# Token sums one period later on VectorE, and a subtraction in four pieces on GpSimd, in a spectral block with a GEGLU

## The chip, the cores and the metric

The kernel runs on one core of one Trainium2 chip. The time is that of one execution on the device, in microseconds (us); smaller is better. The profile is of one execution. TensorE is PE in the profile's rows (PEld its weight loads), VectorE DVE, ScalarE ACT, GpSimd POOL, SyncE SP; L12 is line 12 of the kernel of before.

## The reference

What is computed, cut to its core, for 8192 tokens of 448 channels, with six rows (`sa`, `ca`, `ga`, `sb`, `cb`, `gb`) made of one conditioning vector:

```
h = layernorm(x) * (1 + ca) + sa
x = x + ga * spectral(h)        # rfft over the tokens, a two-layer complex MLP in 4 blocks of
                                # channels, soft shrinkage, inverse rfft
h = layernorm(x) * (1 + cb) + sb
x = x + gb * ((gelu(h @ w_gate) * (h @ w_up)) @ w_down)     # 448 -> 1792 -> 448
```

## The kernel before, in words

The first 700 us transform the tokens, apply the spectral MLP and begin the inverse transform. What follows runs over 32 chunks of 256 tokens (`nch`, 2 blocks of 128 each). For each chunk the inverse's last stage is made (`split_v`, `split_g`, `winverse`), the residual is added and the second layernorm is taken (`norm2` writes tile n), then come gate and up products, the gelu times up, and the down product.

Numbers of more than f16's precision are held as a high and a low part, the low one being the number minus its high part: `split` copies the high part on ScalarE and subtracts on GpSimd. For the inverse's input v (128 x 896 of 32-bit floats, 2 blocks of 448) the copy is `vh`, and the subtraction writes the low part over v itself.

The first 8 chunks (`NSTD`) use plain products for gate and up. Chunks 8 to 31 are the new chunks: gate and up are made by a scheme of seven products of sums (as Strassen and Winograd do it), on the tokens' side by `token_sums`, `wpack_hi` and `wpack_lo`, which form the sums of tile n in tile tf and pack high and low parts into pk. `token_sums` has a part 0 (two subtractions on VectorE, L1326 and L1327, and a copy on GpSimd, L1328) and a part 1 (three subtractions on VectorE, L1330 to L1332).

A new chunk has seven periods (k = 0 to 6), one for each pair of 128 hidden features. The order of the work is written out by hand: each engine takes its instructions in program order, and they wait for each other by semaphores. Period u is made by `period(u)`, and three sets of accumulators in PSUM (`sets`) are used in turn, so that stage A of period u writes the set that period u - 3 used. TensorE's order in a period is stage A of period u (32 matmuls), stage D of u - 2 (12), stage C of u - 1 (24) and stage B of u (10), all at L1385. On the other engines, in the order of the period:

- `seed` (ACT L1417) and what is held over from the period before (`held`: the packing, ACT L1356 and POOL L1362);
- `joins` of u - 2 (DVE L1422 and L1428), which read the accumulators that stage D then goes on to write; the first gelu (ACT L1434);
- `quant_lo` of u - 4 (DVE L1460), the gate products `mult3` (DVE L1438), `copy_b` (ACT L1413);
- behind stage D the second gelu (ACT L1442) and the last gate product `mult1` (DVE L1445), which is the last reader of that set of accumulators;
- the sums of the activations (`sums`, POOL L1191 to L1194), and `quant_hi` of u - 3 (ACT L1450), which reads them.

Behind a period stands the chunk's side work of the table `extra`: after k = 0 `split_v` (ACT L114, POOL L116) for the chunk two ahead, after k = 1 `split_g`, after k = 3 and k = 4 the two parts of `token_sums`; packing goes to `held` and so into the period that follows. After k = 2 `phase` puts the inverse and the seven down products (L1215 to L1217) of the chunk before on TensorE; the last add of these on VectorE is L1270, and GpSimd's are L1229, L1230 and L1261. Weights of the gate and up products come by DMA from SP in each period (L1301).

Of the kernel before, what the change touches and what calls it, by code (L numbers as in the profile page):

```python
# [10 lines left out]
F32 = mybir.dt.float32  # L11
# [5 lines left out]
ALU = mybir.AluOpType  # L17
# [7 lines left out]
CB = 2  # L25
# [15 lines left out]
NSTD = 8  # L41
# [8 lines left out]
def spectral_geglu(ctx, tc, x, w1, b1, w2, b2, wg, wu, wd, cvec, wmod, cf1, cs2, cmi, cgm, out):  # L50
    nc = tc.nc
    V, S, G, T = nc.vector, nc.scalar, nc.gpsimd, nc.tensor
# [59 lines left out]
    def split(hi, lo, src, eh=None, el=None):  # L112

        (eh or S.copy)(hi, src)  # L114
        h = hi.bitcast(F32) if hi.dtype == F32R else hi
        (el or V).tensor_tensor(lo, src, h, ALU.subtract)  # L116
# [883 lines left out]
    with ExitStack() as cctx:  # L1000
# [14 lines left out]
        def each(i):  # L1015

            return [slice(b, b + 1) for b in range(CB)] if i == 0 else [slice(0, CB)]


        halves = [slice(0, HC), slice(HC, D)]  # L1020

        def split_v(i, cs=slice(0, D)):
            n = nxt[i]
            if "vh" not in n:
                n["vh"] = cp.tile([128, CB, D], F32R, tag="vh", name="vh")
                n["vl"] = n["v"].bitcast(F32R)
            for b in each(i):
                split(n["vh"][:, b, cs], n["vl"][:, b, cs], n["v"][:, b, cs], el=G)

# [159 lines left out]
        def sums(x, e):  # L1189
            a12, a11, s1, s2, a22, s3, s4, a21 = (x[:, j] for j in range(8))  # L1190
            e.tensor_tensor(s1, a21, a22, ALU.add)  # L1191
            e.tensor_tensor(s2, s1, a11, ALU.subtract)  # L1192
            e.tensor_tensor(s3, a11, a21, ALU.subtract)  # L1193
            e.tensor_tensor(s4, a12, s2, ALU.subtract)  # L1194
# [82 lines left out]
        NT_, U0 = nch * NP, NSTD * NP  # L1277
# [27 lines left out]
        def after(u, part):  # L1305

            if u in refill:
                pending.append((refill[u], part))

        def flush(keep=()):  # L1310

            for u, part in [p for p in pending if p[1] not in keep]:
                load_part(u, part)
                pending.remove((u, part))
# [84 lines left out]
        def stage_b(u):  # L1399
            mm(u, RY, S2, T2)  # L1400
# [10 lines left out]
        def copy_b(u):  # L1411
            sbs[u] = cp2.tile([128, 2, 256], F32, tag="sb", name="sb", bufs=2)
            S.copy(sbs[u], sets[u % 3][:, :, 0:256])  # L1413
# [50 lines left out]
        def on(u, f):  # L1464
            if U0 <= u < NT_:
                f(u)

        held = []

        def period(u):  # L1470
            on(u, stage_a)
            if u == U0:
                copy_b(u)
                return
            if u == U0 + 1:
                stage_b(U0)
                copy_b(u)
            on(u - 1, seed)
            for fn, *args in held:
                fn(*args)  # L1480
            held.clear()
            on(u - 2, joins)
            on(u - 2, gel3)
            on(u - 4, quant_lo)
            on(u - 2, mult3)
            if u != U0 + 1:
                on(u, copy_b)
            on(u - 2, stage_d)
            on(u - 2, lambda v: after(v, 1))
            on(u - 2, gel1)  # L1490
            on(u - 2, mult1)
            on(u - 2, lambda v: sums(xs[v], G))
            on(u - 3, quant_hi)
            if u == U0 + 1:
                stage_b(u)
                after(U0, 0)
            on(u - 1, stage_c)
            if u != U0 + 1:
                on(u, stage_b)
            on(u, lambda v: after(v, 0))  # L1500
# [12 lines left out]
        def phase(i):  # L1513

            u = i * NP + LA
            pf = sets[(u + 1) % 3]
            j = i + 2
            on(u - 3, quant_lo)
            if j < nch:
                winverse(j, pf)  # L1520
                residual(j)
            steps = {
                0: [(stats2,), (rsqrt_part, 5)],
                1: [(rsqrt_part, 9), (norm2, 0)],
                2: [(norm2, 1)],
            }

            def mid(n):
                for fn, *args in steps[n] if j < nch else []:
                    fn(j, *args)  # L1530

            down(i - 1, down_banks(pf), mid)

        extra = {
            0: [(2, split_v)],
            1: [(2, split_g), (1, wtransposes, [0])],
            2: [(1, wtransposes, range(1, 5))],
# [135 lines left out]
        for n, k in enumerate((4, 7, 11, 13)):  # L1673
# [3 lines left out]
        hooks = {  # L1677
            5: [(1, turn)],
            1: [(2, split_g), (2, split_v)],
            6: [(2, inverse)],  # L1680
            7: [(2, residual)],
# [8 lines left out]
        def later_by_one(k):  # L1690
# [14 lines left out]
        soon = {  # L1705
            0: [(1, token_sums, 0), (1, token_sums, 1), (1, wpack_hi, range(3)), (1, wpack_lo, range(3))],
            1: [(1, wpack_hi, [3, 4]), (1, wpack_lo, [3, 4]), (2, split_g), (2, split_v)],
            5: [(1, turn)],
            6: [(2, inverse)],
# [58 lines left out]
        def store_out():  # L1768
            for i, x1 in outs:
                dma(ov[:, i * CB : (i + 1) * CB, :], x1)  # L1770
            outs.clear()
# [73 lines left out]
        for u in range(U0, NT_ + 1):  # L1845
            period(u)
            i, k = divmod(u, NP)
            if i == nch:
                continue
            if k == LA + 2:  # L1850
                store_out()
            flush()
            for d, fn, *args in opening[k] if i == NSTD and k < 3 else extra[k]:
                if i + d < nch:
                    if fn in (wpack_hi, wpack_lo):
                        held.append((fn, i + d, *args))
                    else:
                        fn(i + d, *args)
            if k == LA:
                phase(i)  # L1860
# [82 lines left out]
```

## Time and profile before

| what | value |
|---|---|
| median of 3 runs | 1890.91 us (1890.71 to 1893.4) |
| the profiled execution's own time | 1890.96 us |
| its span, first to last instruction | 1889.2 us |
| mean granted TensorE clock | 0.996 |
| TensorE busy | 1848.9 us, 98% |
| VectorE, ScalarE, GpSimd busy | 1429.5, 994.4, 1266.7 us |
| DMA | 330.49 MB, 175 GB/s over the span |

In a group's row stand the line, the engine, the operation, the output and inputs by the program's names, the count after an x, then busy time in us and the mean of one in ns, then the engine's idle time before them and what ended it. In a row in order of time stand the start and the duration in us first; a bracket at its end gives idle time ahead of it and what released it.

### The profile page before, as it was taken

To read this page: it belongs to the slowest core of one execution; us is meant where nothing else is said; L and a number is where in the kernel's file an instruction comes from. 1 tells how busy PE (TensorE), PEld (TensorE's weight loads), DVE (VectorE), ACT (ScalarE), POOL (GpSimd) and SP (SyncE) were. 2 spreads that over 40 slices of the span, in tenths; PEclk is the share of its full clock that TensorE was granted. 3 is DMA by queue.
4 is the path that set the end of the run, shared out by engine and by line. 5 is a ranking of instruction groups with operands and counts; after the bars stand their busy time and mean duration, and the time that the engine had idled before them with its cause. 6 is when DMAs were issued, how large, how long until landed. Compare 5 with 4: busy or idle time off the path is not lost.

```text
span 1889.2 us, 56357 instructions
## 1 busy us (share of the span) xinstructions
PE 1848.9 (98%) x23332; PEld 1751.7 (93%) x23332; DVE 1429.5 (76%) x2887; ACT 994.4 (53%) x1844; POOL 1266.7 (67%) x1618
## 2 busy tenths in 40 slices
PE   7899999999999999999999999999999999999998
PEld 3599999878889899999999999999999999999998
DVE  8678788777766667777777777777777777777655
ACT  5677888653444444454554555544554455444443
POOL 3157654347777778777777777777777777777534
PEclk9999999999999999999999999999999999999999
DMA  9999777654544445966666666666666666666651
GB/s 353 316 298 264 205 177 193 185 160 95 133 103 98 99 93 127 296 176 170 169 168 168 168 168 168 168 168 170 177 174 173 169 174 176 176 174 168 162 163 55
DMA packets 380614, 330.49 MB, mean 175 GB/s; under 512 B 110784, under 2 KB 358724, under 8 KB 380356
## 3 DMA queue, kind: packets, MB, share of 16 engines
q1 hardware_dynamic: 380356, 326.87, 63.5%
q8 instruction: 183, 3.00, 0.7%
q14 instruction: 75, 0.61, 0.1%
HBM read 243.32 MB, written 60.10 MB: 161 GB/s over the span
## 4 chain that ended last, share of the span: by engine, by line
PE 77%; DVE 9%; DMA 4%; issue 3%; ACT 3%; POOL 2%; SPq 2%; ACTq 0%; POOLq 0%; DVEq 0%
PE set L1385 34%; PE pgu L1142 10%; PE pdn L1217 6%; PE pdn L1215 6%; PE pdn L1216 6%; PE set L1217 2%; PE set L1216 2%; PE set L1215 2%; DMA xt<-in_A_x 2%; PE ps L211 1%; DVE y L479 1%; DVE x L1438 1%; DVE c L1422 1%; DVE tf L1326 1%; POOL yl L116 1%
## 5 line engine op out<-in xcount | busy, mean ns | idle before, releaser
L1385 PE MATMUL set<-nt,wk 128*128 128x128 f16 x13104 | 742.9, 219 | 3.7 <-DMA wk<-wk 1.6
L1385 PEld LDWEIGHTS <-wk 128*128 128x128 f16 x13104 | 735.6, 98 | 8.9 <-issue 4.8
L1217 PE MATMUL pdn<-wd,ac 128*128 128x224 f16 x1218 | 315.5, 259 | 0.6 <-DVE ac L1203 0.6
L1215 PE MATMUL pdn<-wd,ac 128*128 128x224 f16 x1218 | 315.7, 259 | 0.0
L1216 PE MATMUL pdn<-wd,ac 128*128 128x224 f16 x1218 | 315.5, 259 | 0.0
L1142 PE MATMUL pgu<-nt,wk 128*128 128x256 f16 (+1 forms) x2464 | 269.0, 274 | 3.3 <-DVE x L1183 3.3
L1142 PEld LDWEIGHTS <-wk 128*128 128x128 f16 (+1 forms) x2464 | 226.1, 98 | 44.7 <-issue 18.8
L1434 ACT ACTIVATE gl<-c,dg 128x384 f32<-128x384 f32 x168 | 103.4, 616 | 255.2 <-DVE c L1428 254.2
L1460 DVE SCALAR_TENSOR_TENSOR ac<-x,sa_act,ac 128x896 f16<-128x896 f32 x168 | 212.2, 1263 | 14.7 <-ACT ac L1450 14.7
L1191 POOL TENSOR_TENSOR x<-x 128x128 f32<-128x128 f32 x223 | 130.4, 585 | 120.2 <-DVE x L1183 57.7
L1261 POOL TENSOR_TENSOR cq<-cq 128x224 f32<-128x224 f32 x32 | 21.0, 657 | 262.6 <-DVE cq L1260 262.6
L1438 DVE TENSOR_TENSOR x<-c,gl 128x384 f32<-128x384 f32 x168 | 177.0, 1054 | 17.0 <-ACT gl L1434 17.0
L1450 ACT ACTIVATE ac<-x,sa_act 128x896 f16<-128x896 f32 x168 | 173.5, 1033 | 4.0 <-DVE x L1194 1.3
L1194 POOL TENSOR_TENSOR x<-x 128x128 f32<-128x128 f32 x223 | 170.0, 762 | 0.0
L1215 PEld LDWEIGHTS <-ac 128*128 128x128 f16 x1568 | 153.4, 98 | 4.9 <-issue 4.8
L1217 PEld LDWEIGHTS <-ac 128*128 128x128 f16 x1568 | 153.4, 98 | 0.8 <-DVE ac L1203 0.8
L1216 PEld LDWEIGHTS <-ac 128*128 128x128 f16 x1568 | 153.5, 98 | 0.1
L1193 POOL TENSOR_TENSOR x<-x 128x128 f32<-128x128 f32 x223 | 148.5, 666 | 0.0
L1422 DVE TENSOR_TENSOR c<-set,sb 128x512 f32<-128x512 f32 x168 | 114.9, 684 | 36.1 <-PE set L1385 36.1
L1178 ACT ACTIVATE gel<-pgu,dg 128x256 f32<-128x256 f32 x112 | 49.4, 470 | 158.0 <-PE pgu L1142 150.4
L479 DVE SCALAR_TENSOR_TENSOR y<-pm,t 64x224 f32<-64x224 f32 x256 | 99.5, 389 | 39.1 <-ACT t L471 35.5
L1192 POOL TENSOR_TENSOR x<-x 128x128 f32<-128x128 f32 x223 | 116.9, 524 | 17.5
(336 smaller groups left out, 3987.1 us busy)
## 6 DMA issues: line engine op xcount, KB each, us to landing
wk<-wk SPq DMA_DIRECT2D x76, 1024.0 KB
wk<-wk SPq DMA_DIRECT2D x76, 768.0 KB
vd<-us SPq DMA_DIRECT2D x64, 224.0 KB
xx<-in_A_x SPq DMA_DIRECT2D x32, 448.0 KB
v<-vd SPq DMA_DIRECT2D x63, 224.0 KB
out<-x SPq DMA_DIRECT2D x31, 448.0 KB
xt<-in_A_x SPq DMA_DIRECT2D x15, 896.0 KB
tr<-td SPq DMA_DIRECT2D x60, 224.0 KB
```

Of the source, the lines that this page charges most:

```text
L1142: T.matmul(pgu[i, t, q][:, pr * H : (pr + 1) * H], ws[rows, n, w, tw], nts[i][rows, tn, :], start=start, stop=stop, skip_group_check=True,)
L1191: e.tensor_tensor(s1, a21, a22, ALU.add)
L1193: e.tensor_tensor(s3, a11, a21, ALU.subtract)
L1194: e.tensor_tensor(s4, a12, s2, ALU.subtract)
L1215: T.matmul(ps, ac[:, 0, ka], w[:, 0, kb], start=n == 0, stop=False)
L1216: T.matmul(ps, ac[:, 0, ka], w[:, 1, kb], start=False, stop=False)
L1217: T.matmul(ps, ac[:, 1, ka], w[:, 0, kb], start=False, stop=n == NP - 1)
L1385: T.matmul(ps2[:, pr, reg * 128 : reg * 128 + 128], slot[:, pr, hl, wt, :], nt[:, xt, :], start=start and j == 0, stop=j == len(terms) - 1 ...
L1422: V.tensor_tensor(c[:, :, 1:3, :], p[:, :, 0:256].rearrange("p g (r c) -> p g r c", r=2), b[:, :, 0:128].rearrange("p g (o c) -> p g o c", ...
L1438: V.tensor_tensor(xs[u][:, 1::3, :], cts.pop(u)[:, 1], gls.pop(u), ALU.mult)
L1450: S.activation(ac[:, 0], xs[u][:, 0:7], AF.Copy, scale=sa_act[:, t : t + 1])
L1460: V.scalar_tensor_tensor(ac[:, 1], xs.pop(u)[:, 0:7], sa_act[:, t : t + 1], ac[:, 0], op0=ALU.mult, op1=ALU.subtract)
```

## The change

Two edits, both for the new chunks alone. The two parts of `token_sums` are no longer put behind the period after which `extra` names them, but into a list, `trail`, that the next period empties behind its joins and its gate products, ahead of its sums. The first new chunk's opening is left as it was. And for chunks from 10 on, `split_v` subtracts in four GpSimd instructions of 224 columns (2 blocks times 2 halves) where it had one of 896; the copy to `vh` stays one.

```
@@ split_v
+            if i > NSTD + 1:
+                S.copy(n["vh"], n["v"])
+                for b in range(CB):
+                    for c in halves:
+                        G.tensor_tensor(n["vl"][:, b, c], n["v"][:, b, c], n["vh"][:, b, c].bitcast(F32), ALU.subtract)
+                return
             for b in each(i):
                 split(n["vh"][:, b, cs], n["vl"][:, b, cs], n["v"][:, b, cs], el=G)
@@ period
-        held = []
+        held, trail = [], []
...
             on(u - 2, mult1)
+            for fn, *args in trail:
+                fn(*args)
+            trail.clear()
             on(u - 2, lambda v: sums(xs[v], G))
@@ the loop over the periods
-                    if fn in (wpack_hi, wpack_lo):
+                    if fn is token_sums and u > U0:
+                        trail.append((fn, i + d, *args))
+                    elif fn in (wpack_hi, wpack_lo):
                         held.append((fn, i + d, *args))
```

TensorE's, ScalarE's and SP's instructions stand in the same order in both kernels. On VectorE, from the gate products of period 3 of a new chunk on, there stood in the kernel before (c is the joins' output, x the gate products', ac what `quant_lo` writes):

```order
L1438 TENSOR_TENSOR x_21087<-c,gl_21085 128x3x128
L1445 TENSOR_TENSOR x_21087<-set_11305,gl_21103 128x128
L1326 TENSOR_TENSOR tf<-n_20950 128x192
L1327 TENSOR_TENSOR tf<-n_20950 128x192
L1422 TENSOR_TENSOR c<-set_11303,sb 128x2x256
L1428 TENSOR_TENSOR c<-set_11303,sb 128x2x128
L1460 SCALAR_TENSOR_TENSOR ac<-x_20786,sa_act,ac 128x896
L1438 TENSOR_TENSOR x_21195<-c,gl_21192 128x3x128
L1445 TENSOR_TENSOR x_21195<-set_11303,gl_21211 128x128
L1330 TENSOR_TENSOR tf<-n_20950,tf 128x192
L1331 TENSOR_TENSOR tf<-n_20950,tf 128x192
L1332 TENSOR_TENSOR tf<-n_20950 128x64
```

At the same place of VectorE's order in the changed kernel, whose lines are 6 to 12 higher (L1444 and L1451 are the gate products, L1428 and L1434 the joins, L1466 `quant_lo`, L1332 and L1333 part 0 of the token sums):

```order
L1444 TENSOR_TENSOR x_21120<-c,gl_21118 128x3x128
L1451 TENSOR_TENSOR x_21120<-set_11305,gl_21136 128x128
L1428 TENSOR_TENSOR c<-set_11303,sb 128x2x256
L1434 TENSOR_TENSOR c<-set_11303,sb 128x2x128
L1466 SCALAR_TENSOR_TENSOR ac<-x_20819,sa_act,ac 128x896
L1444 TENSOR_TENSOR x_21224<-c,gl_21221 128x3x128
L1451 TENSOR_TENSOR x_21224<-set_11303,gl_21240 128x128
L1332 TENSOR_TENSOR tf<-n_20983 128x192
L1333 TENSOR_TENSOR tf<-n_20983 128x192
L1428 TENSOR_TENSOR c<-set_11304,sb 128x2x256
L1434 TENSOR_TENSOR c<-set_11304,sb 128x2x128
```

Part 0 has moved from ahead of the joins of period 4 to ahead of those of period 5. Right behind those rows, through period 5 and into period 6, VectorE has now (L1336 to L1338 are part 1):

```order
L1466 SCALAR_TENSOR_TENSOR ac<-x_21120,sa_act,ac 128x896
L1444 TENSOR_TENSOR x_21330<-c,gl_21327 128x3x128
L1451 TENSOR_TENSOR x_21330<-set_11304,gl_21346 128x128
L1336 TENSOR_TENSOR tf<-n_20983,tf 128x192
L1337 TENSOR_TENSOR tf<-n_20983,tf 128x192
L1338 TENSOR_TENSOR tf<-n_20983 128x64
L1428 TENSOR_TENSOR c<-set_11305,sb 128x2x256
```

Part 1 has moved from ahead of the joins of period 5 to ahead of those of period 6. On GpSimd, around period 1 of a new chunk, the kernel before had the sums of one period, the subtraction for v, and the sums of the next:

```order
L1194 TENSOR_TENSOR x_22437<-x_22437 128x128
L116 TENSOR_TENSOR v<-v,vh 128x896
L1191 TENSOR_TENSOR x_22539<-x_22539 128x128
L1192 TENSOR_TENSOR x_22539<-x_22539 128x128
L1193 TENSOR_TENSOR x_22539<-x_22539 128x128
```

There the changed kernel has on GpSimd:

```order
L1200 TENSOR_TENSOR x_22473<-x_22473 128x128
L1031 TENSOR_TENSOR v<-v,vh 128x224 x4
L1197 TENSOR_TENSOR x_22578<-x_22578 128x128
L1198 TENSOR_TENSOR x_22578<-x_22578 128x128
L1199 TENSOR_TENSOR x_22578<-x_22578 128x128
```

The one instruction has become four in its place. Part 0's copy on GpSimd (L1328, now L1334) has moved too, from ahead of the three packing subtractions that follow period 3 to behind them.

## The prediction

> **What bounds the kernel now.** I read the page first, then the waits of TensorE in the new chunks (from 760 us on), then the chain, then the rows of one chunk in order of time.
>
> ```profile
> span 1889.2 us, 56357 instructions
> PE 1848.9 (98%) x23332; PEld 1751.7 (93%) x23332; DVE 1429.5 (76%) x2887; ACT 994.4 (53%) x1844; POOL 1266.7 (67%) x1618
> ```
> ```profile
> PE set L1385 <- DMA wk<-wk: 1.6, 1, 1.6
> PE set L1385 <- ACT sb L1413: 0.6, 1, 0.6
> PE set L1385 <- DVE c L1428: 0.6, 1, 0.6
> ```
>
> The second fence is all that TensorE's matmuls are said to wait for after 700 us: three waits, 2.8 us. Yet matmuls overlap, so a short hole between two of them counts as busy. The holes show in how many matmuls fit a stretch. These rows of TensorE in order of time give start, length, and count after the x:
>
> ```profile
> 1212.84 18.36 PE L1385 MATMUL set<-nt,wk 128*128 128x128 f16 x326
> 1205.43 30.99 PE L1385 MATMUL set<-nt,wk 128*128 128x128 f16 x546
> 1210.40 2.38 PE L1385 MATMUL set<-nt,wk 128*128 128x128 f16 x36
> 1184.39 2.42 PE L1385 MATMUL set<-nt,wk 128*128 128x128 f16 x38
> ```
>
> One matmul lasts 0.219 us, so the undisturbed first row gives a pitch of (18.36 - 0.22) / 325 = 55.8 ns. The second row is a whole chunk's seven periods: 545 x 0.0558 + 0.22 = 30.63 us, but it took 30.99, so 0.36 us are holes. The third row should take 35 x 0.0558 + 0.22 = 2.17: **hole A, 0.21 us**. The fourth should take 2.28: **hole B, 0.14 us**. Together they are the 0.36 within rounding. A period has 78 matmuls, 4.35 us; its stage A has 32 of them, 1.79 us.
>
> Hole A, at 1211.6, is in period 4 of the chunk (the one with k = 4; period 3 starts with the first matmul of the second row, 1205.43, period 4 at 1209.78). Stage D there is due at 1209.78 + 1.79 = 1211.57 and needs the joins L1422 and L1428 of that period:
>
> ```profile
> 1208.98 0.28 DVE L1445 TENSOR_TENSOR x<-set,gl 128x128 f32<-128x128 f32 x1
> 1208.71 1.33 POOL L1230 TENSOR_TENSOR x<-cq,x 128x448 f32<-128x448 f32 x1
> 1209.18 1.09 DVE L1326 TENSOR_TENSOR tf<-n 128x192 f32<-128x192 f32 x1
> 1210.19 0.61 DVE L1327 TENSOR_TENSOR tf<-n 128x192 f32<-128x192 f32 x1
> 1210.72 0.68 DVE L1422 TENSOR_TENSOR c<-set,sb 128x512 f32<-128x512 f32 x1
> 1211.32 0.41 DVE L1428 TENSOR_TENSOR c<-set,sb 128x256 f32<-128x256 f32 x1
> ```
> ```profile
> 1211.78 24.64 PE set L1385 x436
> 1251.83 0.39 DVE cq L1270
> ```
>
> The joins end at 1211.73, and the chain goes from them to TensorE at 1211.78. Ahead of them stand the two token sums of part 0, 1.54 us from 1209.18 to 1210.72; L1326 ends at 1210.27, 0.23 after POOL's L1230. The chain's next chunk shows the same place 46.20 us on (its add L1270 at 1251.83 answers to one at 1205.63).
>
> Hole B, at 1185.5, is at the start of period 2. Its stage A writes the accumulators that the last gate product L1445 of period 1 reads:
>
> ```profile
> 1181.79 1.28 DVE L1460 SCALAR_TENSOR_TENSOR ac<-x,sa_act,ac 128x896 f16<-128x896 f32 x1
> 1182.08 2.94 POOL L116 TENSOR_TENSOR v<-v,vh 128x896 fp32r<-128x896 f32 x1
> 1183.00 2.45 DVE L1438 TENSOR_TENSOR x<-c,gl 128x384 f32<-128x384 f32 x1
> 1183.93 0.37 ACT L1442 ACTIVATE gl<-set,dg 128x128 f32<-128x128 f32 x1
> 1185.37 0.28 DVE L1445 TENSOR_TENSOR x<-set,gl 128x128 f32<-128x128 f32 x1
> 1185.52 0.46 POOL L1191 TENSOR_TENSOR x<-x 128x128 f32<-128x128 f32 x1 [0.50 <-DVE x L1438]
> 1212.81 0.59 DVE L1438 TENSOR_TENSOR x<-c,gl 128x384 f32<-128x384 f32 x1
> ```
>
> L1438 takes 0.59 us at 1212.81 and 2.45 here: it ends at 1185.45, 0.43 after the POOL operation on v ends (1185.02). It stood still for that operation. The operation itself waited for L1460 to end at 1183.07, and then ran some 1.95 us. So DVE's and POOL's operations between SBUF tiles exclude each other for their whole length. The Trainium skill states this (SBUF — State Buffer, section Who interferes with whom): a VectorE instruction with two SBUF inputs and a GpSimd one that reads SBUF hold the shared ports for a whole instruction, and the loser blocks. These rows agree.
>
> **The change part by part.** The two groups over the new chunks, and a POOL operation of 224 columns:
>
> ```profile
> L1326 DVE TENSOR_TENSOR tf<-n 128x192 f32<-128x192 f32 x22 | 23.9, 1086 | 0.0
> L116 POOL TENSOR_TENSOR v<-v,vh 128x896 fp32r<-128x896 f32 x21 | 61.8, 2944 | 0.0
> L1261 POOL TENSOR_TENSOR cq<-cq 128x224 f32<-128x224 f32 x22 | 14.5, 657 | 219.4 <-DVE cq L1260 219.4
> ```
>
> *Hole A removed.* Without part 0 ahead of them, the joins of period 4 start when TensorE's stage C is done. In period 6, which starts at 1205.43 + 3 x 4.35 + 0.21 = 1218.70, they start at 1218.34 straight behind PE, 0.36 before the period:
>
> ```profile
> 1218.34 0.69 DVE L1422 TENSOR_TENSOR c<-set,sb 128x512 f32<-128x512 f32 x1 [0.20 <-PE set L1385]
> ```
>
> So in period 4 they run from 1209.42 to 1210.43 (1.01 us for both), 1.1 us before stage D is due. Stage D then waits for nothing but stage A, on TensorE itself. 22 token sums: 22 x 0.208 = **4.6 us off**.
>
> *Where the sums go.* Joins may start up to 1.79 - 1.01 - 0.05 = 0.73 us after their period's start before stage D waits. Part 0 now stands behind the last gate product of period 4, ahead of the joins of period 5; part 1 one period later. The gate product L1445 starts 3.11 us into an undisturbed period (1188.81, in the period that began at 1185.69, which is 1218.70 - 46.20 + 3 x 4.35 + 0.14), so it ends 3.40 in:
>
> ```profile
> 1188.81 0.29 DVE L1445 TENSOR_TENSOR x<-set,gl 128x128 f32<-128x128 f32 x1 [0.21 <-ACT gl L1442]
> 1213.52 0.34 DVE L1330 TENSOR_TENSOR tf<-n,tf 128x192 f32<-128x192 f32 x1
> 1213.89 0.47 DVE L1331 TENSOR_TENSOR tf<-n,tf 128x192 f32<-128x192 f32 x1
> 1214.28 0.69 DVE L1332 TENSOR_TENSOR tf<-n 128x64 f32<-128x64 f32 x1
> 1214.90 0.68 DVE L1422 TENSOR_TENSOR c<-set,sb 128x512 f32<-128x512 f32 x1
> ```
>
> Part 0: from 1209.78 + 3.33 = 1213.11 (the next DVE operation starts 0.07 before an end). At its old 1.54 us the joins of period 5 start at 1214.65; they are due by 1214.13 + 0.73 = 1214.86. Margin 0.21, and the old price held the wait for L1230, which is long over by then; two operations at L1330's 0.34 are the other end, 0.7 us, and I expect about 1.2. Part 1: from 1217.46, at its old 1.38 us (1213.52 to 1214.90), gives 1218.84 against 1218.48 + 0.73 = 1219.21. **Margin 0.37**, the thinnest that rests on an unseen encounter: POOL's work beside it is other than before. The ends: 0.7 us less (no stop at all, and no gain, since TensorE has nothing to gain there), or each of the three stopped for a whole POOL operation:
>
> ```profile
> 1217.48 0.99 POOL L1362 TENSOR_TENSOR pk<-n,pk 128x256 f16<-128x256 f32 x1
> 1218.43 0.45 POOL L1191 TENSOR_TENSOR x<-x 128x128 f32<-128x128 f32 x1
> ```
>
> that is 0.99 + 0.45 + 0.45, and 0.25 us each to run (from L1326's 0.23 behind L1230): 2.64 us, 0.89 late. I take the old price, nearest in kind: cost 0. ScalarE's casts of the tf pieces stand a period behind each part still, and POOL's copy into tf changes places with three pk operations: the same POOL work ahead of the same sums; it is hidden behind TensorE's periods.
>
> *Hole B removed.* The first of four pieces starts when L1460 ends, at 1183.02, and takes about 0.6 us; L1438, asked for at 1183.00, then runs 0.45 and ends near 1184.1. Its follower L1445 then waits only for ScalarE's L1442, 1184.30, and ends at 1184.6, 0.9 us before stage A needs it. 21 x 0.136 = **2.9 us off**. On POOL, four pieces cost 4 x 0.657 = 2.63 in place of some 1.95 to 2.1, and L1438 now runs between them (0.45): the last ends near 1185.8 in place of 1185.02. The 0.50 us that POOL sat idle before L1191 hides about two thirds; the sums, which ended at 1188.18, come some 0.3 us later, and ScalarE takes them at 1188.68. The inverse on TensorE reads v at 1190.31. Cost 0; were that cover gone, ScalarE's copy would come as much later, and nothing on TensorE hangs on it within the period.
>
> ```profile
> 1186.88 1.30 POOL L1194 TENSOR_TENSOR x<-x 128x128 f32<-128x128 f32 x1
> 1188.68 1.03 ACT L1450 ACTIVATE ac<-x,sa_act 128x896 f16<-128x896 f32 x1
> 1190.31 0.19 PEld L1508 LDWEIGHTS set<-v,gh 128*128 128x128 f32 x1
> ```
>
> *Sum.* 4.6 + 2.9 = 7.4 us (unrounded) off the profiled execution, 1890.96 us, whose span is 1889.2; it stands 0.05 over the median of the runs, 1890.91. **1883.5 us.** DMAs, their order on SP, TensorE's and ScalarE's orders stay.
>
> **The rivals.** (1) *The hole moves to period 6*: part 1 makes its joins some 0.2 us late, as hole A was. 22 x 0.2 = 4.4 back: 1887.9. For: POOL's pk operation of 0.99 us and two sums stand just there. Against: a margin of 0.37 at the old price. (2) *Three full stops*: each operation of part 1 meets a POOL operation from its start, 0.89 late: 22 x 0.89 = 19.6, 1903.1. It is slower than before from 0.34 us late on. For: L1327 and L1326 were both stopped. Against: L1330 was not, and three full stops in a row are in no row here. The skill's section named above lets this happen, as it has no share of the port, only a whole instruction. (3) *POOL keeps the port over its four pieces*, so L1438 waits for all, 0.6 + 3 x 0.657 = 2.57 us in place of the single operation's 1.95, 0.62 more: 21 x 0.62 = 13.0 on, 4.6 off: 1899.4. Against it:
>
> ```profile
> 1220.34 0.81 DVE L1438 TENSOR_TENSOR x<-c,gl 128x384 f32<-128x384 f32 x1
> 1220.70 0.77 POOL L1194 TENSOR_TENSOR x<-x 128x128 f32<-128x128 f32 x1
> ```
>
> L1438 runs there among POOL's sums, which follow each other without a break, and the sum behind it takes 0.77 in place of L1191's 0.45. (4) *The split does nothing for hole B*: 1886.4.
>
> **How the numbers follow.** Forecast 0.62; rival (1) 0.18; (2) 0.06; (3) 0.05; (4) 0.09. A measurement of this kernel tells about 0.2%, 3.8 us, from no change: below 1887.1 is faster, above 1894.7 slower. The forecast and (4) are faster, 0.71; (1) is within, 0.18; (2) and (3) are slower, 0.11. The range goes from 1882.8 (both holes slightly larger than read) to 1889.0, which takes in (4) and (1) up to a hole of 0.25 us; what is left out is (2), (3) and the rest of (1).
>
> **What would show it.** Seven periods in one row of 546 matmuls in 30.6 us, and chunks 45.86 us apart in place of 46.20. L1422 of period 4 about 0.36 before its period, with PE as its releaser. L1438 beside the four pieces about 1.1 us in place of 2.45. Joins of period 6 no later than 0.73 us into it: if they are later, rival (1) or (2). A row of 2.28 us for 38 matmuls at the start of period 2; if 2.42 or more, rival (3) or (4). The prediction is wrong if the gaps of TensorE go where I did not look, as at the down products.

## The result, and the profile after

| | before | after |
|---|---|---|
| median of 5 runs | 1891.38 us (1890.71 to 1893.4) | 1883.83 us (1882.79 to 1884.1) |
| the profiled execution | 1890.96 us | 1882.79 us |
| its span | 1889.2 us | 1881.0 us |

The ratio is 0.9958, 95% interval 0.9947 to 0.997: 7.6 us less by the medians, 0.4%, and the interval lies clear of no change. The profiled executions differ by 8.17 us; 0.8 of that lies ahead of the new chunks, whose first matmul started at 761.3 us before and at 760.5 after, where nothing was changed.

The page and the waits of TensorE show next to nothing, as before. These are the page's first two rows and all waits of matmuls after 700 us:

```profile
span 1881.0 us, 56421 instructions
PE 1841.5 (98%) x23332; PEld 1748.9 (93%) x23332; DVE 1397.2 (74%) x2887; ACT 1000.7 (53%) x1844; POOL 1271.3 (68%) x1684
```
```profile
PE set L1391 <- DMA wk<-wk: 1.6, 1, 1.6
PE set L1391 <- ACT sb L1419: 0.6, 1, 0.6
PE set L1391 <- DVE c L1434: 0.6, 1, 0.6
```

The gain is in how closely the matmuls stand. One chunk's seven periods as a row in order of time (start, length, count), and the same chunk in the chain of work, with its neighbour:

```profile
1201.63 30.65 PE L1391 MATMUL set<-nt,wk 128*128 128x128 f16 x546
```
```profile
1155.93 30.48 PE set L1391 x546
1201.79 30.48 PE set L1391 x546
```

30.65 us in place of 30.99: both holes are gone, and chunks follow each other in 1201.79 - 1155.93 = 45.86 us in place of 46.20. The chain says the same in another way. Before, it left TensorE in 14 of the 22 chunks that have hole A, for the last add of the down products and VectorE's joins, gate product and token sums; in the other 8 it shows hole A only as a pause of some 0.04 us. Now it stays on TensorE for all 546 matmuls of every chunk, since nothing else ends last. The same reading of all chunks, by the starts of their matmuls: before, hole A stands in 22 chunks, 0.21 us in the mean, and hole B in 21, 0.13 us, 7.4 us together; after, none of them has a hole.

Hole A's place, period 4 of this chunk (1201.63 + 4.35 = 1205.98), and VectorE behind it:

```profile
1205.63 0.69 DVE L1428 TENSOR_TENSOR c<-set,sb 128x512 f32<-128x512 f32 x1 [0.17 <-PE set L1391]
1206.23 0.41 DVE L1434 TENSOR_TENSOR c<-set,sb 128x256 f32<-128x256 f32 x1
1209.31 0.35 DVE L1332 TENSOR_TENSOR tf<-n 128x192 f32<-128x192 f32 x1
1209.58 0.58 DVE L1333 TENSOR_TENSOR tf<-n 128x192 f32<-128x192 f32 x1
1210.08 0.68 DVE L1428 TENSOR_TENSOR c<-set,sb 128x512 f32<-128x512 f32 x1
1213.66 0.66 POOL L1368 TENSOR_TENSOR pk<-n,pk 128x256 f16<-128x256 f32 x1
1213.66 0.87 DVE L1336 TENSOR_TENSOR tf<-n,tf 128x192 f32<-128x192 f32 x1
1214.57 0.50 DVE L1337 TENSOR_TENSOR tf<-n,tf 128x192 f32<-128x192 f32 x1
1214.99 0.47 DVE L1338 TENSOR_TENSOR tf<-n 128x64 f32<-128x64 f32 x1
1215.39 0.68 DVE L1428 TENSOR_TENSOR c<-set,sb 128x512 f32<-128x512 f32 x1
```

The joins of period 4 start 0.35 us before their period, and what they waited for is TensorE (the bracket). Part 0 takes 0.77 us (1209.31 to 1210.08). Part 1 takes 1.73 (1213.66 to 1215.39), and the joins behind it start 0.70 us into period 6 (1201.63 + 3 x 4.353 = 1214.69).

Hole B's place, period 1 (GpSimd's four pieces are merged into one row):

```profile
1223.98 1.42 DVE L1466 SCALAR_TENSOR_TENSOR ac<-x,sa_act,ac 128x896 f16<-128x896 f32 x1
1224.42 3.70 POOL L1031 TENSOR_TENSOR v<-v,vh 128x224 fp32r<-128x224 f32 x4
1225.33 1.02 DVE L1444 TENSOR_TENSOR x<-c,gl 128x384 f32<-128x384 f32 x1
1226.52 0.29 DVE L1451 TENSOR_TENSOR x<-set,gl 128x128 f32<-128x128 f32 x1 [0.17 <-ACT gl L1448]
```

The gate product beside the pieces takes 1.02 us where it took 2.45. The last gate product now waits for ScalarE and ends at 1226.81, 0.95 us before period 2 (1201.63 + 6 x 4.353 = 1227.75). Behind the pieces, the last of GpSimd's sums of period 2, and ScalarE's `quant_hi` right behind it:

```profile
1230.49 0.45 POOL L1200 TENSOR_TENSOR x<-x 128x128 f32<-128x128 f32 x1
1230.97 1.04 ACT L1456 ACTIVATE ac<-x,sa_act 128x896 f16<-128x896 f32 x1
```

### The profile page after: what moved, and what is told of

Same layout as the page of the kernel before. It is cut to its first block, busy times and chain, and to the rows that moved or that the text cites. A ratio compares the mean times of both kernels' runs of the same rounds, so it can differ in the third digit from the quotient of the medians.

```text
span 1881.0 us, 56421 instructions
## 1 busy us (share of the span) xinstructions
PE 1841.5 (98%) x23332; PEld 1748.9 (93%) x23332; DVE 1397.2 (74%) x2887; ACT 1000.7 (53%) x1844; POOL 1271.3 (68%) x1684
## 4 chain that ended last, share of the span: by engine, by line
PE 82%; DVE 6%; DMA 3%; issue 3%; ACT 2%; SPq 2%; POOL 2%; ACTq 0%; DVEq 0%; POOLq 0%
PE set L1391 39%; PE pgu L1148 11%; PE pdn L1221 6%; PE pdn L1223 6%; PE pdn L1222 6%; PE ps L211 2%; PE set L1223 2%; PE set L1222 2%; PE set L1221 2%; DVE y L479 1%; POOL yl L116 1%; DVE st L172 1%; PE set L1515 1%; DMA raw<-in_B_w_gate 1%; DVE wk L838 1%
## 5 line engine op out<-in xcount | busy, mean ns | idle before, releaser
L1466 DVE SCALAR_TENSOR_TENSOR ac<-x,sa_act,ac 128x896 f16<-128x896 f32 x168 | 205.8, 1225 | 19.9 <-ACT ac L1456 19.9
L1197 POOL TENSOR_TENSOR x<-x 128x128 f32<-128x128 f32 x223 | 129.8, 582 | 117.6 <-DVE x L1189 56.2
L1198 POOL TENSOR_TENSOR x<-x 128x128 f32<-128x128 f32 x223 | 185.6, 832 | 17.5
L1444 DVE TENSOR_TENSOR x<-c,gl 128x384 f32<-128x384 f32 x168 | 154.4, 919 | 17.2 <-ACT gl L1440 17.1
L1428 DVE TENSOR_TENSOR c<-set,sb 128x512 f32<-128x512 f32 x168 | 115.4, 687 | 35.7 <-PE set L1391 35.7
L1199 POOL TENSOR_TENSOR x<-x 128x128 f32<-128x128 f32 x223 | 134.0, 601 | 0.0
L1419 ACT COPY sb<-set 128x512 f32<-128x512 f32 x168 | 97.6, 581 | 61.8 <-PE set L1391 60.4
```

The lines of the kernel that those rows point to most:

```text
L1444: V.tensor_tensor(xs[u][:, 1::3, :], cts.pop(u)[:, 1], gls.pop(u), ALU.mult)
L1466: V.scalar_tensor_tensor(ac[:, 1], xs.pop(u)[:, 0:7], sa_act[:, t : t + 1], ac[:, 0], op0=ALU.mult, op1=ALU.subtract)
```

## The experiments

All are compared with the kernel before, run on the same chip, 1891.1 to 1891.3 us there. For each, the row of one chunk is read against the changed kernel's 30.65 us.

**Each edit alone.** The sums moved, v's low part in one operation:

```
-            if i > NSTD + 1:
+            if False:
                 S.copy(n["vh"], n["v"])
```

> The token sums moved as in the change, v's low part in one operation of 896 columns as before. Theory (two holes of TensorE per chunk, each with one cause): hole A, 0.21 us, is gone, hole B, 0.14 us at the start of period 2, is there as before, 21 times: 2.9 us more than the changed kernel, about 1886.7 us; the gate product beside the operation on v still takes some 2.4 us. Rival (the holes are coupled, and one edit does the work of both): 1883.8 us with no hole at period 2, or a larger hole than 0.14.

The pieces alone:

```
-                    if fn is token_sums and u > U0:
+                    if False:
```

> The four pieces as in the change, the token sums where they were before. Theory: hole B is gone, hole A, 0.21 us in period 4, is there as before, 22 times: 4.6 us more than the changed kernel, about 1888.4 us. Rival (coupled holes): 1883.8 us, or 1891 us if the pieces help only behind the moved sums.

The chunk rows, of the sums alone and of the pieces alone:

```profile
1204.43 30.91 PE L1391 MATMUL set<-nt,wk 128*128 128x128 f16 x546
```
```profile
1205.64 30.84 PE L1391 MATMUL set<-nt,wk 128*128 128x128 f16 x546
```

The pieces alone: 1888.49 us (ratio 0.9991, 0.9982 to 0.9999). Hole A is there, 30.84 - 30.65 = 0.19 (0.20 in the mean of all chunks), and hole B is gone: as the theory said. The sums alone: 1889.27 us (0.9992, 0.9984 to 1.0001), where 1886.7 was expected. Hole A is gone, but hole B is 0.26 us in place of 0.14, which is the larger hole that the rival named. Before, the last of GpSimd's sums ahead of the operation on v stood here:

```profile
1181.67 0.46 POOL L1194 TENSOR_TENSOR x<-x 128x128 f32<-128x128 f32 x1
```

Period 1 and the start of period 2 with the sums alone:

```profile
1226.79 1.41 DVE L1466 SCALAR_TENSOR_TENSOR ac<-x,sa_act,ac 128x896 f16<-128x896 f32 x1
1226.80 0.45 POOL L1200 TENSOR_TENSOR x<-x 128x128 f32<-128x128 f32 x1
1227.21 2.95 POOL L116 TENSOR_TENSOR v<-v,vh 128x896 fp32r<-128x896 f32 x1
1228.12 2.45 DVE L1444 TENSOR_TENSOR x<-c,gl 128x384 f32<-128x384 f32 x1
1230.50 0.28 DVE L1451 TENSOR_TENSOR x<-set,gl 128x128 f32<-128x128 f32 x1
```

L1466 takes 1.41 us where the same operation of before (1181.79, shown with the prediction) took 1.28. Before, it started 0.12 us after that sum and stood still until the sum ended; now it starts together with the sum (L1200) and stands still for all of it. All behind it, the operation on v and the gate product, is that much later. So the two edits do not add up as terms: alone they are worth 1.8 and 2.6 us by the medians, together 7.6. The interval of the sums alone takes in no change, so their time by itself shows little; what is read here rests on the rows.

**What makes hole B larger.** My first theory was that part 1, which now ends late, delays GpSimd's sums from period 6 on. The sums moved alone, with the subtraction of 64 columns in part 0:

```
                 V.tensor_tensor(t3, b22, b12, ALU.subtract)
                 G.tensor_copy(t[:, 576:640], x1)
+                V.tensor_tensor(t[:, 832:896], x0, x1, ALU.subtract)
...
                 V.tensor_tensor(t4, b21, t2, ALU.subtract)
-                V.tensor_tensor(t[:, 832:896], x0, x1, ALU.subtract)
```

> As the kernel with the token sums moved alone (v's low part in one operation), and the subtraction of 64 columns taken from part 1 into part 0, which has 1 us to spare. With the sums moved alone hole B was 0.27 us in place of 0.14. Theory (part 1 ends so late that GpSimd's sums of period 6 start 0.13 us later against TensorE, and the operation on v with them): part 1 is some 0.45 us shorter, GpSimd is in time again, hole B is back at 0.14 us, 21 x 0.13 = 2.7 us less than with the sums moved alone, about 1886.5 us. Rival (hole B is larger because TensorE, without hole A, is 0.21 us earlier at period 2, wherever part 1 ends): hole B stays at 0.27 us, 1889.3 us.

```profile
1203.81 30.93 PE L1391 MATMUL set<-nt,wk 128*128 128x128 f16 x546
```
```profile
1226.16 1.44 DVE L1466 SCALAR_TENSOR_TENSOR ac<-x,sa_act,ac 128x896 f16<-128x896 f32 x1
1226.19 0.46 POOL L1200 TENSOR_TENSOR x<-x 128x128 f32<-128x128 f32 x1
```

1889.58 us (0.9992, 0.9983 to 1.0001), hole B 0.28. The theory fell; its rival had 0.27. The next one: GpSimd works nearly without a pause from the end of the down products to the operation on v (before, 26.16 us busy, time in which it stands still for VectorE included, of the 26.90 from 1204.40 to 1231.30), so the place of its sums is set by its own queue, and TensorE without hole A is 0.21 us ahead of it.

```profile
1204.40:1231.30 26.90, 26.16 (x34) 1.00 0.45 139
```

Two kernels take work from that queue. The first puts part 0's copy on ScalarE:

```
-                G.tensor_copy(t[:, 576:640], x1)
+                (G.tensor_copy if i <= NSTD + 1 else S.copy)(t[:, 576:640], x1)
```

> The token sums moved alone (v's low part in one operation), with part 0's copy of 64 columns on ScalarE in place of GpSimd. Theory (GpSimd works without a pause from the end of the down products to the operation on v, so its queue sets when that operation ends, and hole B is larger than before because TensorE is 0.21 us earlier): 0.23 us less on GpSimd brings hole B from 0.27 to 0 to 0.1 us, 4 to 5.6 us less than with the sums moved alone, 1883.8 to 1885.5 us. Rival (GpSimd's operations are set by where VectorE's quantization stops them, once per period, so a small relief is lost at the next stop): hole B stays at 0.2 to 0.27 us, 1888 to 1889.5 us.

The second leaves out a packing subtraction of 256 columns in period 5:

```
             for k in ks:
+                if i > NSTD + 1 and k == 2:
+                    continue
```

> The token sums moved alone, and GpSimd's low part of one piece of pk (256 columns, 0.67 to 0.78 us in period 5 of a chunk) left out in the chunks from 10 on, so that part of the products is not what the reference computes. Theory (GpSimd's queue): 0.7 us less ahead of the operation on v, hole B is gone, 1883.8 us within 1.5. Rival (the place of the stops): hole B of 0.14 to 0.27 us stays, 1886.5 to 1889.5 us.

The chunk rows, with the copy on ScalarE and with the subtraction left out:

```profile
1204.25 30.83 PE L1391 MATMUL set<-nt,wk 128*128 128x128 f16 x546
```
```profile
1205.01 30.82 PE L1393 MATMUL set<-nt,wk 128*128 128x128 f16 x546
```

1887.98 us (0.9982, 0.9973 to 0.9992) and 1888.17 us (0.9984, 0.9976 to 0.9993); hole B is 0.18 and 0.17. With the copy on ScalarE that lies between what theory and rival gave. With the subtraction left out it is what the rival gave, and the theory, by which the hole would be gone, missed. Less work for GpSimd does make hole B smaller, by some 0.09 us, so its queue has a part in it. But leaving out 0.7 us does no more for it than leaving out 0.23. The rows show one reason: GpSimd does not work without a pause there. First a row of the sums moved alone, in period 6, then the rows around the start of the sums of period 0 with the subtraction left out:

```profile
1221.37 0.46 POOL L1197 TENSOR_TENSOR x<-x 128x128 f32<-128x128 f32 x1 [0.49 <-DVE x L1444]
```
```profile
1223.66 1.78 POOL L1370 TENSOR_TENSOR pk<-tf,pk 128x512 f16<-128x512 f32 x1 [0.19 <-ACT pk L1362]
1224.34 1.51 DVE L1446 TENSOR_TENSOR x<-c,gl 128x384 f32<-128x384 f32 x1
1225.93 0.45 POOL L1197 TENSOR_TENSOR x<-x 128x128 f32<-128x128 f32 x1 [0.49 <-DVE x L1446]
```

With the sums alone GpSimd stands idle for 0.49 us until the gate product L1444 is done, in 20 of the 21 chunks with hole B; so there its place is not set by its own queue alone. (With the 64 columns moved it has no such stop, and hole B is as large.) With the subtraction left out it is free at 1225.44 and stands idle once more until the gate product L1446 is done, which GpSimd's own packing operation had stopped. What it gained is lost at the next gate product that it waits for.

What the size of hole B does go with, in all these kernels, is the end of the last sum ahead of the operation on v. With the copy on ScalarE and with the subtraction left out it stands here:

```profile
1226.54 0.46 POOL L1200 TENSOR_TENSOR x<-x 128x128 f32<-128x128 f32 x1
```
```profile
1227.29 0.45 POOL L1200 TENSOR_TENSOR x<-x 128x128 f32<-128x128 f32 x1
```

In the mean over the chunks the sum ends 0.91 us into period 1 before, 0.96 with the subtraction left out, 0.97 with the copy on ScalarE, 1.05 with the sums alone and 1.06 with the 64 columns moved; hole B is 0.13, 0.18, 0.19, 0.27 and 0.28 us. What sets that end when hole A is gone, and how much of the 0.21 us comes back in general, stays open.

**Two pieces.** The changed kernel with v's low part in two operations of 448 columns:

```
-                    for c in halves:
-                        G.tensor_tensor(n["vl"][:, b, c], n["v"][:, b, c], n["vh"][:, b, c].bitcast(F32), ALU.subtract)
+                    G.tensor_tensor(n["vl"][:, b], n["v"][:, b], n["vh"][:, b].bitcast(F32), ALU.subtract)
```

> The changed kernel with v's low part in two operations of 448 columns in place of four of 224. Theory (only the end of the last gate product of period 1 against the start of period 2 counts): the first piece lasts about 1.05 us once it has the port, the gate product beside it ends some 0.5 us later than beside a piece of 224, about 0.8 us before TensorE needs it: no hole, 1883.8 us within 1 us. Rival (the wait shrinks with the length of a piece and TensorE feels it): half of hole B stays, 21 x 0.07 = 1.4 us more, 1885.2 us.

```profile
1204.62 30.65 PE L1390 MATMUL set<-nt,wk 128*128 128x128 f16 x546
```
```profile
1228.31 1.50 DVE L1443 TENSOR_TENSOR x<-c,gl 128x384 f32<-128x384 f32 x1
1229.73 0.28 DVE L1450 TENSOR_TENSOR x<-set,gl 128x128 f32<-128x128 f32 x1
```

1884.51 us (0.9969, 0.9956 to 0.9981) and no hole. The gate product is stopped half a microsecond longer, 1.50 in place of 1.02, and ends the chain early enough all the same: period 2 begins at 1204.62 + 26.12 = 1230.74, the last gate product is done at 1230.01. The time lies as near to the theory's as to the rival's, but the row shows no hole, as the theory had it. Four pieces are not better than two by these rows.

**The limit for the joins.** Part 0 alone moved, so that all five operations stand ahead of the joins of period 5:

```
-                    if fn is token_sums and u > U0:
+                    if fn is token_sums and u > U0 and args == [0]:
```

> Only part 0 of the token sums is moved by a period, part 1 stays where it was, so that all five operations stand between the last gate product of period 4 and the joins of period 5. Theory (joins may start 0.73 us after the period's start): part 0 took 0.77 us in the changed kernel and part 1 takes 1.4 to 1.7, so the joins of period 5 start 0.4 to 0.75 us too late; 22 x that is 9 to 16 us more than the changed kernel, 1893 to 1900 us, and the hole moves to period 5. Rival (what pays is that period 4, behind the down products, is relieved): 1883.8 us.

One more operation in part 1:

```
                 V.tensor_tensor(t4, b21, t2, ALU.subtract)
+                if i > NSTD + 1:
+                    V.tensor_tensor(t4, b21, t2, ALU.subtract)
```

> The changed kernel with one more VectorE subtraction in part 1 of the token sums (the one that writes t4, made twice with the same result). Part 1 now stands ahead of the joins of period 6, which start 0.70 us into it in the changed kernel's profile. Theory (0.73 us is the limit, so 0.03 us is left): the operation takes 0.34 to 0.5 us, a hole of 0.3 to 0.47 us opens in period 6 of 22 chunks, 6.6 to 10.3 us more than the changed kernel, 1890 to 1894 us. Rival (the margin of 0.37 us as the prediction had it): a hole of 0 to 0.13 us, 1884 to 1887 us.

Part 0 alone, then the extra operation: the chunk now falls into two rows, and the bracket is the part of the hole in which no matmul was under way.

```profile
1208.55 10.66 PE L1391 MATMUL set<-nt,wk 128*128 128x128 f16 x188
1218.53 0.68 DVE L1428 TENSOR_TENSOR c<-set,sb 128x512 f32<-128x512 f32 x1
1219.60 20.15 PE L1391 MATMUL set<-nt,wk 128*128 128x128 f16 x358 [0.39 <-DVE c L1434]
```
```profile
1205.99 15.02 PE L1393 MATMUL set<-nt,wk 128*128 128x128 f16 x266
1220.28 0.68 DVE L1430 TENSOR_TENSOR c<-set,sb 128x512 f32<-128x512 f32 x1
1221.34 15.79 PE L1393 MATMUL set<-nt,wk 128*128 128x128 f16 x280 [0.33 <-DVE c L1436]
```

Part 0 alone: 1895.83 us (1.0027, 1.0016 to 1.0038), slower than before, with the hole in period 5. That period starts at 1208.55 + 2 x 4.353 = 1217.26, the joins are due at 1217.99 and start at 1218.53, 0.54 late. Without a hole the second row's first matmul would start 188 x 0.0558 = 10.49 us after the first's; it starts 11.05 after: a hole of 0.56. The extra operation: 1894.06 us (1.0015, 1.0006 to 1.0024). Period 6 starts at 1219.05, the joins are due at 1219.78 and start at 1220.28, 0.50 late; the hole is 15.35 - 266 x 0.0558 = 0.51. 22 times 0.56 and 0.51 are 12.3 and 11.2 us; the medians are 12.0 and 10.2 above the changed kernel's. The limit of 0.73 us holds in both, to 0.02. The hole of the extra operation and its time lie just above what the theory gave, 0.3 to 0.47 us and 1890 to 1894.

The extra operation again, with the subtraction of 64 columns moved into part 0:

> The changed kernel with both: the subtraction of 64 columns in part 0, and t4 made twice in part 1, so that part 1 has three operations as in the changed kernel, the last one of 192 columns in place of 64. Theory (only when part 1 ends counts, not how much VectorE has to do in the chunk): VectorE's work is that of the kernel with one more operation, but part 1 ends at most 0.15 us later than in the changed kernel, a hole of 0 to 0.12 us in period 6, 1884 to 1886.5 us. Rival (one more operation costs where VectorE is behind, wherever it stands): as with the extra operation alone.

```profile
1203.67 30.65 PE L1393 MATMUL set<-nt,wk 128*128 128x128 f16 x546
```

1884.55 us (0.9964, 0.9952 to 0.9977), no hole in this chunk; two of the 22 have one of 0.22 us in period 6. VectorE does the same work as in the kernel above, where it cost 10 us. With one of its operations moved to part 0 it costs 0.7 us by the medians, of which the two holes are 0.4.

**All runs together.** Added up over all chunks of a trace, the holes are 4.4 us with the pieces alone, 5.6 with the sums alone, 5.8 with the 64 columns moved, 3.9 with the copy on ScalarE, 3.8 with the subtraction left out, 12.5 with part 0 alone and 10.7 with the extra operation. Each of these kernels, and the one before with its 7.4, is slower than the changed kernel by its sum to within 0.6 us, by the medians.

## Why the prediction was right, and where it was not

- *What bounds the kernel, hole A, hole B*: right in place, cause and size: without part 0 ahead of the joins hole A is gone, with the pieces hole B is, each in the kernel with that edit alone. The forecast of 7.4 us off stands against 7.6 by the medians and 8.2 by the profiled executions, of which 0.8 is from elsewhere. The chunk's 45.86 us and the joins' start came out as written.
- *The gate product beside the pieces*: about 1.1 us expected, 1.02 measured; the last gate product ends 0.95 us before TensorE needs it, as worked out. Rival (3), that GpSimd keeps the port over its pieces, is out: L1444 ran 1.02 us beside 3.70 us of them.
- *The price of part 0*: about 1.2 us expected, 0.77 measured.
- *The price of part 1*: this step failed. It was taken over from before, 1.38 us, for a margin of 0.37. It measured 1.73, since its first operation met the packing operation of 256 columns and took 0.87 us, and the other two met a sum each. The margin was 0.03 us. Rival (2)'s three stops did come, but shorter than it had them. That the total came out in spite of this is luck: 0.03 us more and rival (1) would have begun. The extra operation shows it: it took back all of the gain.
- *The pieces on GpSimd*: the sums behind them were expected some 0.3 us later. They end 1230.94 - 1227.75 = 3.19 us into period 2, where it was 1188.18 - 1185.69 = 2.49 before, 0.7 later. ScalarE's `quant_hi` starts 0.2 us later, and no hole comes of it: the cost of 0 was right, the cover was smaller than said.
- *The sum as two independent terms*: right only because both edits were made. The sums alone gave 1.8 us where the term was 4.6, since hole B grew to 0.27 us. Rival (4), with hole B left as it was, would have been dearer than its 1886.4: 1889.3 is what that kernel measured.

## What to carry to other kernels

An engine that is 98% busy can still have holes that a list of waits doesn't show; count how many of its instructions fit a stretch, against the pitch in an undisturbed one. Work out for each wait the latest time at which its producer may start, and compare moved work against that limit with the neighbours that it will have there, not with the price that it had at the old place. Between two engines that exclude each other, cut the longer operation only until the other's last result is in time: here two pieces did what four did.

## What the runs showed of the hardware that was not expected

With pieces, VectorE and GpSimd took turns: in the changed kernel and in the one with two pieces, VectorE's waiting operation ran after the first piece, not after the last (1.02 us beside pieces of 224 columns, 1.50 beside 448, 2.45 beside one of 896). And the exclusion couples timing in both directions: with the sums moved alone L1466 started 0.12 us earlier against GpSimd's last sum than before, stood still that much longer, and hole B was 0.13 us larger; and GpSimd in turn stood idle for 0.49 us behind gate products that its own operations had stopped.
